# Weight transfers beside attention: issued by GpSimd's queue instead of SyncE's, with more lead counted for them

## The chip, the cores and the metric

The kernel runs on one core of a Trainium2 chip. Its engines are TensorE (PE, matrix products), VectorE (DVE), ScalarE (ACT), GpSimd (POOL) and SyncE (SP), which only issues transfers. Each engine takes its instructions strictly in the order in which the program has them; engines wait for each other, and for DMAs, on semaphores. 16 DMA engines move the data that any queue issues. The metric is the device time of one execution in microseconds; the median of the runs counts.

## The reference

```
attn = sigmoid(q @ k.T / sqrt(64) - log(448)) @ v         # 4 batches, 12 heads, 448 tokens, head size 64
x    = attn as (1792 tokens, 768)
h    = x @ moe_w_in;   x = elu(h) @ moe_w_out             # 768 -> 2048 -> 768
h    = x @ moe2_w_in;  out = (h - tanh(h)) @ moe2_w_out   # 768 -> 2048 -> 768
```

q, k and v come as float32, the four weights as float64, so a block of 128 x 768 weights is 768 KB.

## The kernel before

**Work.** Attention goes pair by pair of heads, 24 pairs, two of them per load. For a pair PE transposes q and k (`sps`, L309), splits of which ACT (L315) and DVE (L317, L322) write; it computes the scores (`sps`, `spq`, L344), ACT takes the sigmoids (`an`, `a`, L358), PE multiplies with v (`pvps`, L369) and DVE copies the result out (L381). After attention come the two layers. Every product there is made by a scheme with seven products in place of eight, from operands split into a high and a low part: `x_sum` (L702), `x_head` (L712) and `x_rest` (L718) make the operands of x, for tokens s = 0 and s = 1, and `m_p` (L746) runs the products of the first layer.

**Weights beside attention.** A float64 weight is made into float32 in three steps, `narrow_to`: ACT (L541), DVE (L544), DVE (L548). Beside attention this is done for the first four blocks of the first weight (`job(...)` with place 4, n = 0 to 3: `load` into the buffer `R1a`, `narrow`, and for n = 2 and 3 `keep` of the result in DRAM) and for all 16 blocks of the second weight: `p_load` (L592, into `XB` for even j and `XA` for odd j by the trace's names; j = 0 to 7, c = 0 and 1), `p_narrow`, four sums `p_sum` (L601), and two stores `p_store` (L606: 192 KB for c = 0 and 1152 KB for c = 1) into `p_forms` in DRAM. The buffers of j are used again by j + 2: `p_load` of j + 2 waits for the narrowing of j, and its narrowing waits for the stores and sums of j. When the last of this is done, the same space takes the operands of x for s = 0 (`x_head` and `x_rest` into `XB`).

**The order.** The class `Sched` writes the order out ahead of time. Each operation has a queue, a counted cost and a counted latency (`raw_op(key, queue, cost, fn, after, latency)`); operations go by earliest start, then by rank, and those of attention keep their own planned order. On ACT and DVE another operation is put into a gap only if it ends before the next planned one of attention, plus 100 ns. The counts only set the order; on the chip an instruction waits for its data alone. An entry in the list `after` that has no shared data, such as `("s", 1, 0)` for `p_load`, orders only the count.

GpSimd's work in this stretch is eight memsets and the mask `ident` at the start, ended at 3.4 us; its sums of weights (`w_sum`, L661) begin after attention.

Of the kernel before, what the change touches and what calls it, by code (L numbers as in the profile page):

```python
# [11 lines left out]
I32 = mybir.dt.int32  # L12
# [87 lines left out]
def kernel(  # L100
# [20 lines left out]
    nc = tc.nc  # L121
# [5 lines left out]
    SP = S // R  # L127
    NAN, NAF, NVL, NL = 3, 1, 2, 2
    KD = DM // 128
# [6 lines left out]
    DH = DM // 2  # L136
# [31 lines left out]
    with tc.manual_schedule():  # L168
# [246 lines left out]
        def mlp():  # L415
# [42 lines left out]
            def raw_tile(tag, epoch):  # L458

                if (tag, epoch) not in raws:  # L460
                    n = RAW[tag]
                    split = epoch % 2 == 1 and tag != "R1b"
                    raws[tag, epoch] = raw_p.tile([128, n], F32R if split else F32, tag=tag, name=tag)
                return raws[tag, epoch]
# [23 lines left out]
            CW = KD * 128  # L488
# [3 lines left out]
            wide = moe_w_in.dtype != F32  # L492
# [5 lines left out]
            kept, stage_of, in_scratch = {}, {}, set()  # L498
            OPENING = {0: 0, 1: 1} if wide else {}

            def stage(job):
                p, epoch = stage_of[job]
                if p >= 2:
                    return raw_tile(*{2: ("R1b", epoch), 4: ("R1a", 0), 5: ("R1a", 1.5)}[p])[:, :2 * CW]
                return (first[:, :2 * CW], second)[p]
# [7 lines left out]
            def result(job):  # L513
                if job in OPENING:
                    return spare[:, OPENING[job] * CW:(OPENING[job] + 1) * CW]
                return scratch(job) if job in in_scratch else stage(job)[:, :CW]

            def source(key):
                w, i, n = key
                f0 = n * 128  # L520
                if w == "wi":
                    return w_ins[i][:, f0:f0 + 128].bitcast(dt).rearrange("(k p) f -> p k f", p=128)
                return w_outs[i][f0:f0 + 128, :].bitcast(dt).rearrange("p (k f) -> p k f", k=KD)

            def load(job, key, narrowed):
                t = stage(job)
                if narrowed:
                    nc.sync.dma_start(out=t[:, :CW], in_=kept[key])
                elif wide:
                    nc.sync.dma_start(out=t.bitcast(I32).rearrange("p (k f) -> p k f", k=KD), in_=source(key))  # L530
                else:
                    nc.sync.dma_start(out=t[:, :CW].rearrange("p (k f) -> p k f", k=KD), in_=source(key))

# [19 lines left out]
            def keep(job, key):  # L553
                if key[:2] == ("wo", 1):
                    j, c = divmod(key[2], 2)
                    nc.sync.dma_start(out=w_forms()[:, 2 * c:2 * c + 2, j], in_=result(job).rearrange("p (r e) -> p r e", r=2))
                    return
                name = "kept_" + "_".join(map(str, key))
                kept[key] = store_p.tile([128, CW], F32, name=name, tag=name)
                nc.sync.dma_start(out=kept[key], in_=result(job))  # L560

            def w_forms():
                if "wf" not in hidden:
# [13 lines left out]
            def p_part(j, what):  # L577
                lo, hi = ((0, 2 * CW), (2 * CW, 4 * CW), (4 * CW, 5 * CW), (5 * CW, 8 * CW))[what]
                if j % 2 and what < 2:
                    return rooms["XA2"][:, lo:hi]  # L580
                return rooms["XB0"][:, lo + j % 2 * 4 * CW:hi + j % 2 * 4 * CW]
# [7 lines left out]

            def p_load(j, c):  # L590
                if wide:
                    nc.sync.dma_start(out=p_part(j, c).bitcast(I32).rearrange("p (k f) -> p k f", k=KD), in_=source(("wo", 0, 2 * j + c)))  # L592
                else:
                    nc.sync.dma_start(out=p_part(j, 2 + c)[:, :CW].rearrange("p (k f) -> p k f", k=KD), in_=source(("wo", 0, 2 * j + c)))

            def p_narrow(j, c, step):
                narrow_to(step, p_part(j, c), p_part(j, 2 + c)[:, :CW], p_part(j, 2 + c)[:, :CW])
# [5 lines left out]
            def p_store(j, c):  # L603
                t = p_part(j, 2 + c)
                a0, a1 = ((0, 1), (1, 7))[c]
                nc.sync.dma_start(out=p_forms()[:, a0:a1, j], in_=t[:, :(a1 - a0) * DH].rearrange("p (a e) -> p a e", a=a1 - a0))  # L606

            def p_forms():
                if "pf" not in hidden:
                    hidden["pf"] = store_p.tile([128, 7 * NG * DH], F32, name="p_forms", tag="p_forms")  # L610
                return hidden["pf"].rearrange("p (a j e) -> p a j e", a=7, j=NG)
# [205 lines left out]
            def o_order(i, s):  # L817
# [5 lines left out]
            W_SUMS = {"S1": ("A21", "A22", ALU.add), "S2": ("S1", "A11", ALU.subtract),  # L823
                      "S4": ("A12", "S2", ALU.subtract), "S3": ("A11", "A21", ALU.subtract)}
# [127 lines left out]
            def dve(n):  # L952
                return int(1.047 * n) + 150

            def raw_op(key, queue, cost, fn, after, latency=100):
                assert key not in mine, key
                mine[key] = (queue, cost, fn, list(after), latency)

            def op(kind, key, queue, cost, fn, after, latency=100):
                raw_op((kind,) + key, queue, cost, lambda: fn(*key), after, latency)  # L960
# [61 lines left out]
            t = 0  # L1022
# [10 lines left out]
            def job(key, keeps, place, after=(), only=False, i=0):  # L1033

                n = count[0]
                count[0] += 1
                stage_of[n] = (place, 2 * i + 1)
                if only and wide:
                    in_scratch.add(n)
                live = key not in kept_by  # L1040
                after = list(after) + list(stage_frees[place])
                if not live:
                    after.append(("keep", kept_by[key], key))
                raw_op(("load", n), "SP", 600, lambda: load(n, key, not live), after, 8500 if live else 6000)
                done = ("load", n)
                if place == 4:
                    fixed[done] = 3 * CYCLE + n
                free = scratch_free[(0, 0, 1, 2, 2, 3)[place]]
                if live and wide:
                    for step, (queue, cost) in enumerate((("ACT", 910), ("DVE", 560), ("DVE", 970))):  # L1050
                        raw_op(("narrow", n, step), queue, cost, lambda step=step: narrow(n, step),
                               [done] + (free if step == 0 else []), 100)
                        done = ("narrow", n, step)
                        if place == 4:
                            fixed[done] = n * CYCLE
                    free[:] = [done]
                stage_frees[place] = [done]
                if keeps:
                    kept_by[key] = n
                    raw_op(("keep", n, key), "SP", 600, lambda: keep(n, key), [done], 12000 if place == 4 else 5600)  # L1060
                    if n in in_scratch:
                        free[:] = [("keep", n, key)]
                    else:
                        stage_frees[place].append(("keep", n, key))
                return n, done
# [314 lines left out]
            for j in range(NG):  # L1380
                was = [] if j < 2 else [("p_narrow", j - 2, c, 2) for c in range(2)]
                held = [] if j < 2 else [("p_sum", j - 2, x) for x in W_SUMS] + [("p_store", j - 2, c) for c in range(2)]
                for c in range(2):
                    op("p_load", (j, c), "SP", 600, p_load, [("s", 1, 0)] + (was[c:c + 1] if wide else held), 11000)
                    done = ("p_load", j, c)
                    for step, (queue, cost) in enumerate((("ACT", 910), ("DVE", 560), ("DVE", 970)) if wide else ()):
                        op("p_narrow", (j, c, step), queue, cost, p_narrow,
                           [done] + (held if step == 0 else []), 100)
                        done = ("p_narrow", j, c, step)
                    ends_in[c] = done  # L1390
                both = [ends_in[c] for c in range(2)]
                for x in W_SUMS:
                    op("p_sum", (j, x), "DVE", dve(DH), p_sum, both + [("p_sum", j, y) for y in W_SUMS[x][:2] if y in W_SUMS])
                op("p_store", (j, 0), "SP", 600, p_store, both[:1], 8000)
                op("p_store", (j, 1), "SP", 600, p_store, both[1:] + [("p_sum", j, x) for x in W_SUMS], 8000)
            for k in mine:
                if k[0][:2] == "p_":
                    fixed[k] = (2 * k[1] + 2) * CYCLE
# [15 lines left out]
            for k, o in mine.items():  # L1414
                after = [x for a in o[3] for x in joint.get(a, [a])]
# [11 lines left out]
            while todo:  # L1427
                k = todo.pop()
# [47 lines left out]
```

## Time and profile before

| | us |
|---|---|
| median of 3 runs | 1025.57 (1024.84 to 1026.34) |
| the profiled execution | 1025.25 |
| its span, first to last instruction | 1023.5 |
| PE busy, of the span | 990.7 |
| DVE, ACT, POOL busy | 763.9, 600.8, 79.4 |
| mean granted TensorE clock | 0.992 of full speed |

Busy times are sums over the span, in which attention (to about 197 us) and the two layers have different limits; what a change in one stretch is worth is read in that stretch. Times in the rows are us from the start of the span, durations in us unless marked ns.

### The profile page before, as it was taken

The page shows a single profiled execution, that of the slowest core. Times are in us where ns is not written, and L with a number is a line of the kernel's source. Part 1 is how long each engine was busy: PE and PEld are TensorE (multiplying, and loading weights), DVE is VectorE, ACT ScalarE, POOL GpSimd, SP SyncE. Part 2 cuts the span into 40 slices and gives each one's busy share as a digit, 9 for nine tenths or more (in the row PEclk, how much of TensorE's full clock was granted, in tenths as well). Part 3 has the DMA queues.
Part 4 walks back from the last instruction along what each step waited for, and adds up shares of the span by engine and source line. Part 5 has one row for each costly group of instructions (what it writes and reads, how often), then busy time and mean ns, then how long its engine had stood idle before and what let it go on. Part 6 is the DMA issues. An engine that isn't in the chain of part 4 may idle for free.

```text
span 1023.5 us, 15546 instructions
## 1 busy us (share of the span) xinstructions
PE 990.7 (97%) x5300; PEld 855.4 (84%) x5300; DVE 763.9 (75%) x1155; ACT 600.8 (59%) x966; POOL 79.4 (8%) x74
## 2 busy tenths in 40 slices
PE   8969899989999999999999999999999999999998
PEld 6535455678888888888899998888888999999998
DVE  3657677898888888768878789777777779566673
ACT  4746567876666667666667565444444546445652
POOL 0000000012222220000000021111111000000000
PEclk9989899999999999999999999999999999999999
DMA  7889897025555569999994733555555894455442
GB/s 196 240 253 302 250 285 219 16 80 190 189 188 188 188 203 316 380 412 411 345 328 125 247 109 111 191 190 191 187 194 184 304 335 160 136 174 170 125 143 89
DMA packets 171263, 218.61 MB, mean 214 GB/s; under 512 B 58672, under 2 KB 129584, under 8 KB 170928
## 3 DMA queue, kind: packets, MB, share of 16 engines
q1 hardware_dynamic: 169616, 217.04, 63.8%
q8 instruction: 41, 0.67, 0.3%
q10 hardware_dynamic: 1568, 0.59, 0.2%
q14 instruction: 38, 0.31, 0.1%
HBM read 142.61 MB, written 74.97 MB: 213 GB/s over the span
## 4 chain that ended last, share of the span: by engine, by line
PE 89%; DMA 5%; DVE 3%; ACT 1%; issue 1%; SPq 1%; ACTq 0%; DVEq 0%
PE psa L746 12%; PE psd L746 11%; PE psx L746 9%; PE psu L901 7%; PE psv L901 7%; PE psw L901 7%; PE pvps L369 6%; PE psa L901 6%; PE psb L901 6%; PE psb L746 5%; PE psy L901 4%; PE sps L344 3%; PE psx L901 3%; DMA p_forms<-XB 2%; PE sps L309 2%; DMA R1a<-in_moe_w_in_dram 1%
## 5 line engine op out<-in xcount | busy, mean ns | idle before, releaser
L358 ACT ACTIVATE an<-sps,bias 128x896 f32<-128x896 f32 x72 | 67.3, 1005 | 34.1 <-PE sps L344 33.9
L873 ACT ACTIVATE XB<-t 128x384 fp32r<-128x384 f32 (+1 forms) x111 | 62.0, 563 | 40.8 <-PE psw L901 11.7
L877 DVE TENSOR_TENSOR XB<-t,XB 128x384 fp32r<-128x384 f32 (+1 forms) x111 | 68.3, 625 | 13.2 <-ACT XB L873 13.0
L661 POOL TENSOR_TENSOR second<-second 128x384 f32<-128x384 f32 x15 | 19.0, 1269 | 709.1 <-DVE second L548 213.6
L369 PE MATMUL pvps<-an,vl 128*64 128x448 f32 x288 | 62.7, 573 | 0.0
L873 ACT ACTIVATE XB<-spare 128x512 fp32r<-128x512 f32 (+1 forms) x72 | 41.1, 572 | 26.9 <-PE psw L901 6.6
L344 PEld LDWEIGHTS sps<-e 64*128 64x128 f32 x432 | 39.9, 189 | 18.9 <-PE pvps L369 15.5
L746 PE MATMUL psa<-XB,W 128*128 128x512 f32 x192 | 54.2, 391 | 0.0
L344 PE MATMUL sps<-e 64*128 64x448 f32 x432 | 51.3, 380 | 0.0
L877 DVE TENSOR_TENSOR XB<-spare,XB 128x512 fp32r<-128x512 f32 (+1 forms) x72 | 44.2, 621 | 9.2 <-ACT XB L873 8.8
L901 PE MATMUL psu<-XB,XB 128*128 128x384 f32 (+1 forms) x192 | 46.3, 348 | 0.0
L901 PE MATMUL psv<-XB,XB 128*128 128x384 f32 (+1 forms) x192 | 46.2, 348 | 0.0
L901 PE MATMUL psw<-XB,XB 128*128 128x384 f32 (+1 forms) x192 | 46.2, 348 | 0.0
L369 PEld LDWEIGHTS pvps<-an,vl 128*64 128x64 f32 x288 | 19.5, 144 | 28.5 <-issue 21.1
L746 PEld LDWEIGHTS psa<-XB,W 128*128 128x128 f32 x192 | 36.0, 188 | 7.5
L775 ACT ACTIVATE spare<-t 128x512 f32<-128x512 f32 (+1 forms) x33 | 19.0, 579 | 37.2 <-DVE t L763 36.1
L661 POOL TENSOR_TENSOR first<-first,second 128x384 f32<-128x384 f32 x30 | 40.1, 1335 | 1.2
L317 DVE CAST e<-sps 128x448 fp32r<-128x448 f32 x24 | 15.0, 624 | 30.4 <-PE sps L309 19.3
L746 PE MATMUL psd<-XB,W 128*128 128x512 f32 x144 | 35.7, 391 | 1.5 <-DVE W L678 1.3
L779 ACT ACTIVATE spare<-spare 128x512 f32<-128x512 f32 (+1 forms) x64 | 36.6, 572 | 0.7
L901 PE MATMUL psa<-XB,XB 128*128 128x384 f32 (+1 forms) x156 | 36.9, 347 | 0.0
L901 PE MATMUL psb<-XB,XB 128*128 128x384 f32 (+1 forms) x156 | 36.9, 347 | 0.0
(362 smaller groups left out, 2717.7 us busy)
## 6 DMA issues: line engine op xcount, KB each, us to landing
x_forms<-R1b SPq DMA_DIRECT2D x58, 256.0 KB, 2.0
first<-p_forms SPq DMA_DIRECT2D x36, 384.0 KB, 6.1
t<-x_forms SPq DMA_DIRECT2D x64, 192.0 KB, 2.9
t<-x_forms SPq DMA_DIRECT2D x47, 256.0 KB, 5.0
x_forms<-t SPq DMA_DIRECT2D x44, 256.0 KB, 2.0
x_forms<-R1b SPq DMA_DIRECT2D x58, 192.0 KB, 4.8
first<-in_moe_w_in_dram SPq DMA_DIRECT2D x14, 768.0 KB, 5.3
second<-in_moe_w_in_dram SPq DMA_DIRECT2D x14, 768.0 KB, 6.2
```

The source lines that it names most:

```text
L309: nc.tensor.transpose(ps[:, c * P:(c + 1) * P], t[:, c, h:h + 2, :], ident[:P, :P])
L317: nc.vector.tensor_copy(out=to, in_=x)
L344: nc.tensor.matmul(out=ps[:, j, :S], lhsT=e[lanes, ks, cols], rhs=e[lanes, qs, :S], start=(x == 0), stop=(x == 2),)
L358: nc.scalar.activation(out=a[:, :m], in_=T.pop(("s", n, u))[:, :m, :S], func=ACTF.Sigmoid, bias=bias, scale=scale)
L369: nc.tensor.matmul(out=ps[D * j:D * j + D], lhsT=vl[n // NL % NVL][:, n % NL, 5 * j + u if u < 3 else 3 + j], rhs=a[:, j if u < 3 else 0], ...
L661: by.tensor_tensor(out=out, in0=x, in1=y, op=op)
L746: nc.tensor.matmul(out=ps, lhsT=w[wz][:, k0:k0 + 128], rhs=xs[xz][:, kk], start=(opens and n == 0), stop=(n == 3 * KH - 1), skip_group_che ...
L775: nc.scalar.activation(out=r, in_=h, func=ACTF.Tanh)
L779: nc.scalar.activation(out=r, in_=r, func=ACTF.Exp, scale=-1.0)
L873: nc.scalar.activation(out=at_place(og_place[i, s, p, j], 0, i)[:, :HW[s]], in_=T["graw", i, s, p, j], func=ACTF.Copy)
L877: nc.vector.tensor_tensor(out=lo, in0=T.pop(("graw", i, s, p, j)), in1=f(hi), op=ALU.subtract)
L901: nc.tensor.matmul(out=T["o2", tag], lhsT=lhsT, rhs=rhs, start=(p in OPENS and j == 0 and x == 0), stop=(j == NG - 1 and x == 2), skip_gro ...
```

## The change

The 4 loads and 2 keeps with place 4 and all `p_load` and `p_store` are issued by `nc.gpsimd` instead of `nc.sync`. In the order they stand on the queue POOL with a cost of 1500 instead of 600, and with longer latencies: 14000 instead of 8500 for the loads with place 4, 12000 instead of 11000 for `p_load`, 9000 instead of 8000 for `p_store`. The loads and stores of q, k, v, of everything after attention, and the two loads that bring the kept blocks back stay on SyncE.

```
             def load(job, key, narrowed):
                 t = stage(job)
+                by = nc.gpsimd if stage_of[job][0] == 4 else nc.sync
...
-                    nc.sync.dma_start(out=t.bitcast(I32).rearrange("p (k f) -> p k f", k=KD), in_=source(key))
+                    by.dma_start(out=t.bitcast(I32).rearrange("p (k f) -> p k f", k=KD), in_=source(key))
...
             def keep(job, key):
...
-                nc.sync.dma_start(out=kept[key], in_=result(job))
+                (nc.gpsimd if stage_of[job][0] == 4 else nc.sync).dma_start(out=kept[key], in_=result(job))
...
             def p_load(j, c):
-                    nc.sync.dma_start(out=p_part(j, c).bitcast(I32)..., in_=source(("wo", 0, 2 * j + c)))
+                    nc.gpsimd.dma_start(out=p_part(j, c).bitcast(I32)..., in_=source(("wo", 0, 2 * j + c)))
...
             def p_store(j, c):
-                nc.sync.dma_start(out=p_forms()[:, a0:a1, j], in_=...)
+                nc.gpsimd.dma_start(out=p_forms()[:, a0:a1, j], in_=...)
...
-                raw_op(("load", n), "SP", 600, lambda: load(n, key, not live), after, 8500 if live else 6000)
+                raw_op(("load", n), *(("POOL", 1500) if place == 4 else ("SP", 600)), lambda: load(n, key, not live), after, 14000 if place == 4 else 8500 if live else 6000)
...
-                    raw_op(("keep", n, key), "SP", 600, lambda: keep(n, key), [done], 12000 if place == 4 else 5600)
+                    raw_op(("keep", n, key), *(("POOL", 1500) if place == 4 else ("SP", 600)), lambda: keep(n, key), [done], 12000 if place == 4 else 5600)
...
-                    op("p_load", (j, c), "SP", 600, p_load, [("s", 1, 0)] + (was[c:c + 1] if wide else held), 11000)
+                    op("p_load", (j, c), "POOL", 1500, p_load, [("s", 1, 0)] + (was[c:c + 1] if wide else held), 12000)
...
-                op("p_store", (j, 0), "SP", 600, p_store, both[:1], 8000)
-                op("p_store", (j, 1), "SP", 600, p_store, both[1:] + [("p_sum", j, x) for x in W_SUMS], 8000)
+                op("p_store", (j, 0), "POOL", 1500, p_store, both[:1], 9000)
+                op("p_store", (j, 1), "POOL", 1500, p_store, both[1:] + [("p_sum", j, x) for x in W_SUMS], 9000)
```

## Rows read from the trace of the kernel before

**Rows 1.** Page, part 1: busy time, share of the span, instructions of each engine.
```profile
PE 990.7 (97%) x5300; PEld 855.4 (84%) x5300; DVE 763.9 (75%) x1155; ACT 600.8 (59%) x966; POOL 79.4 (8%) x74
```

**Rows 2.** Chain of waits, 0 to 240 us: start, duration, what.
```profile
5.57 3.71 DMA first<-in_q_dram
...
15.18 3.16 PE pvps L369 x16
...
55.18 13.80 DMA R1a<-in_moe_w_in_dram
...
72.70 3.96 PE pvps L369 x16
...
91.83 9.74 DMA p_forms<-XB
...
108.27 11.31 DMA p_forms<-XB
...
168.58 3.16 PE pvps L369 x16
...
175.41 3.16 PE pvps L369 x16
...
194.21 3.18 PE pvps L369 x16
```

**Rows 3.** Windows: stretch, its length, busy time per engine, granted clock, DMA share, GB/s.
```profile
6.00:9.00 3.00, 1.67 (x12) 1.25 (x12) 1.27 (x3) 1.06 (x2) 0.00 (x0) 1.00 0.92 213
...
56.00:60.00 4.00, 4.00 (x26) 1.83 (x23) 3.23 (x6) 3.14 (x5) 0.00 (x0) 1.00 1.04 399
...
68.00:72.00 4.00, 1.16 (x6) 1.16 (x7) 2.08 (x4) 3.00 (x4) 0.00 (x0) 0.50 0.56 126
...
80.00:100.00 20.00, 19.96 (x131) 11.45 (x129) 15.91 (x28) 13.81 (x19) 0.00 (x0) 1.00 0.95 292
...
200.00:222.60 22.60, 18.49 (x90) 15.80 (x88) 22.46 (x39) 17.89 (x35) 5.12 (x4) 1.00 0.15 53
```

**Rows 4.** Waits, 0 to 245 us: total us, times, longest us.
```profile
POOL second L661 <- DVE XB L718: 199.6, 1, 199.6
...
ACT R1b L541 <- DMA R1a<-in_moe_w_in_dram: 12.0, 2, 9.2
ACT XB L541 <- DMA p_forms<-XB: 11.8, 4, 5.3
...
ACT XB L541 <- DMA XA<-in_moe_w_out_dram: 4.2, 2, 2.8
```

**Rows 5.** Timeline of SyncE's queue: start, duration, what, count.
```profile
19.95 1.45 SPq L592 DMA_DIRECT2D XB<-in_moe_w_out_dram  x2
...
56.31 9.98 SPq L234 DMA_DIRECT2D kq<-in_q_dram  x4
```

**Rows 6.** Timeline of PE, 190 to 245 us; in brackets the idle time before.
```profile
222.59 0.62 PE L746 MATMUL psd<-XB,R0a 128*128 128x384 f32 x2 [3.25 <-ACT R1b L758]
```

**Rows 7.** Timeline of DVE, 155 to 245 us.
```profile
161.81 0.62 DVE L317 CAST e<-sps 128x448 fp32r<-128x448 f32 x1 [0.69 <-PE sps L309]
163.10 1.22 DVE L322 TENSOR_TENSOR e<-sps,e 128x512 fp32r<-128x512 f32 x2 [0.66 <-ACT e L315]
165.01 0.63 DVE L381 COPY R1a<-pvps 128x448 f32<-128x448 f32 x1 [0.68 <-PE pvps L369]
...
172.36 1.88 DVE L718 TENSOR_TENSOR XB<-R0a,XB 128x512 fp32r<-128x512 f32 x3
```

**Rows 8.** Lines L606 and L234: durations of an issue in ns, min/median/max.
```profile
L606 SPq DMA_DIRECT2D p_forms<-XB x16: 378/539/1522, 38.9 to 166.1; - x16
...
L234 SPq DMA_DIRECT2D first<-in_q_dram x20: 435/816/3688, 12.3 to 147.2; - x20
```

**Rows 9.** DMA issues: count, KB each, median us from issue to landing.
```profile
p_forms<-XB SPq DMA_DIRECT2D x8, 1152.0 KB, 8.9
...
R1a<-in_moe_w_in_dram SPq DMA_DIRECT2D x4, 768.0 KB, 9.0
```

More of the change, by code (lines that the diff above doesn't have):

```diff
@@ L591, in p_load @@
                 if wide:
-                    nc.sync.dma_start(out=p_part(j, c).bitcast(I32).rearrange("p (k f) -> p k f", k=KD), in_=source(("wo", 0, 2 * j + c)))
+                    nc.gpsimd.dma_start(out=p_part(j, c).bitcast(I32).rearrange("p (k f) -> p k f", k=KD), in_=source(("wo", 0, 2 * j + c)))
                 else:
-                    nc.sync.dma_start(out=p_part(j, 2 + c)[:, :CW].rearrange("p (k f) -> p k f", k=KD), in_=source(("wo", 0, 2 * j + c)))
+                    nc.gpsimd.dma_start(out=p_part(j, 2 + c)[:, :CW].rearrange("p (k f) -> p k f", k=KD), in_=source(("wo", 0, 2 * j + c)))
             def p_narrow(j, c, step):
@@ L605, in p_store @@
                 a0, a1 = ((0, 1), (1, 7))[c]
-                nc.sync.dma_start(out=p_forms()[:, a0:a1, j], in_=t[:, :(a1 - a0) * DH].rearrange("p (a e) -> p a e", a=a1 - a0))
+                nc.gpsimd.dma_start(out=p_forms()[:, a0:a1, j], in_=t[:, :(a1 - a0) * DH].rearrange("p (a e) -> p a e", a=a1 - a0))
             def p_forms():
```

## The prediction, made before the result was known

> **What bounds the kernel now.** I read the page's busy table first: TensorE (PE) is busy 97% of the span, so only a stretch where it stands idle can give time back [rows 1]. The chain of waits shows where that is. Attention has a fixed beat: the `pvps` group of one pair of heads starts 6.83 us after that of the pair before (168.58 to 175.41); the last three beats take 18.80 together, since the last two pairs have no transposes beside them. The first group starts at 15.18, the last at 194.21. Undisturbed this takes 20 x 6.83 + 18.8 = 155.4 us; it took 179.0, so 23.6 us are lost. The same view names what stands there: DMAs of 13.80, 9.74 and 11.31 us, all of them weight transfers [rows 2]. A deep loss is followed by a slow group: with a granted clock of 0.50 in 68 to 72 us (1.2 instead of 2.4 GHz, after PE had stood still) the group at 72.70 took 3.96 instead of 3.16 [rows 2, 3]. That is inside the 23.6.
>
> The table of waits says how a late weight stops attention. ACT takes its work in the written order; it waits 12.0 us for `R1a` (loads of the first layer's weight), 11.8 for `p_forms` (stores of the second weight's parts, whose buffer the next narrowing writes) and 4.2 for `XA` (loads of the second weight), 28.0 in all [rows 4]. The sigmoids behind these narrowings come late, and so does PE.
>
> Why are they late? SyncE's own timeline shows one line for everything. The load into `R1a` issued at 55.18 lands 13.80 us later; the four q loads behind it hold SyncE for 9.98 us, where one takes 0.82 in the median [rows 2, 5, 8]. The DMA engines are full while weights flow (share 1.04 in 56 to 60 us) and half empty just after (0.56 in 68 to 72) [rows 3].
>
> After attention DVE is the bound: it is busy 22.46 of the 22.6 us ahead of 222.6 [rows 3], making operands for the first products. PE's last long stand (3.25 us) ends at 222.59 [rows 6]. This DVE work can begin only when the second weight has left the buffer `XB`; its first instruction `XB<-R0a` stands at 172.36 [rows 7]. So the end of the passage hangs on two things: when attention ends, and when the weights have left `XB`.
>
> **The change, part by part.**
>
> *Moved issues.* 4 loads and 2 keeps of the first weight, 16 loads and 16 stores of the second leave SyncE's queue for GpSimd's: 38 instructions. A store costs SyncE 0.54 us in the median [rows 8], so at most some 20 us of its time in all; SyncE bounds nothing, so this alone is worth nothing. What it buys is that q, k and v no longer queue behind weights, nor weights behind q, k and v.
>
> *GpSimd's cost of an issue.* No row shows GpSimd issuing a transfer. The nearest from below is a store's shortest issue on SyncE, 0.38 us; from above, the longest of all there, 3.69 us, a q load held up by a full queue [rows 8]. I take 0.54, that of the same store. Up to 3.69 it costs nothing: from the last memset (3.4 us) 38 issues behind each other and 8.9 us of landing [rows 9] end at 3.4 + 38 x 3.69 + 8.9 = 152.5 us, before the 167.6 that I come to below. What hides it is that GpSimd has nothing else to do: it sits idle for 199.6 us there [rows 4]. Above that the cover is gone, and GpSimd's pace sets the end (last rival).
>
> *Early issues.* The order holds the first loads of the second weight back until the scores of pair 1, but only on paper: their buffers are fresh, so no data makes them wait. On SyncE they stood behind all the first q, k and v loads and left at 19.95 [rows 5]. GpSimd has nothing in front of them, so load 0 of the first weight and then both halves of `p_load` 0 leave from 3.4 us on; load 1 stands behind narrowing 0 and holds back the rest. That is 3 x 768 KB = 2.36 MB into a stretch where the DMA engines have a share of 0.92 at 213 GB/s [rows 3], while PE waits for its first q load (5.57 to 9.28) [rows 2]. If that load keeps its time the cost is 0; if all 2.36 MB pass first, it is 8.1 us at the 292 GB/s of the slice 80 to 100 us [rows 3]. With equal shares, and weights flowing from 4.9 us, the 0.93 MB that passed until 9.28 would take as much of the weights along: 4 us, which I take.
>
> *More lead.* In the order a narrowing now stands 1500 + 12000 instead of 600 + 11000 ns behind its load, 1500 + 9000 instead of 600 + 8000 behind the store that frees its buffer (1.9 us more each), and 15.5 instead of 9.1 us behind a load of the first weight. The measured landings are 9.0 us for that load and 8.9 for the large store in the median [rows 9], so the new counts cover the usual case, though not all of a pile-up like 13.80 [rows 2]. ACT has one gap per beat for these, so a narrowing moves by no gap or by one. Two chains of three store-to-narrowing steps run interleaved (j = 0, 2, 4, 6 and 1, 3, 5, 7), so the weights leave `XB` 0 to 3 beats (0 to 20.5 us) later in the order. I take one beat, 6.8 us.
>
> *Stalls that remain.* The bytes are the same, so the engines stay near full; of 23.6 us I keep 8 (bounds 2, one short hold-up, and 23.6). Late next are the q and k loads: after 9.98 us of waiting for issue they would have been late too.
>
> *Sum.* Attention's last group lasts 3.1 us [rows 2], so attention ends at 15.2 + 155.4 + 4 + 8 + 3.1 = 185.7. The weights leave `XB`: all 23.6 us were lost ahead of 172.36, so undisturbed at 148.8; plus 6.8 + 4 + 8 = 167.6. From there DVE needed 50.2 us to the end of PE's stand (172.4 to 222.6). Attention's own share of DVE is 0.62 + 1.22 + 0.63 = 2.47 us per beat, 36% [rows 7]; it ran beside for 24.9 us before and 18.1 now, which saves 6.8 x 0.36 = 2.5. So PE goes on at 167.6 + 50.2 - 2.5 = 215.3 instead of 222.6: 7.3 us less. The profiled execution took 1025.25 us, its span of 1023.5 and 1.75 around it, 0.3 below the median of the runs (1025.57); 1025.3 - 7.3 = 1018.0.
>
> **Rivals.** *Better: the lead costs nothing.* If every narrowing finds its old gap and only 3 us of stalls remain, `XB` is free at 148.8 + 7 = 155.8 and attention ends at 180.7, both 16.6 us earlier: 1008.7. For it: the waits it must hide sum to 28 us, but few are long [rows 2, 4]. Against it: it needs the same bytes through in less time.
>
> *No change: the DMA engines were the bound.* In the slice from 80 to 100 us the share is 0.95 [rows 3]. If that is the limit, two queues move the bytes no faster, the same waits return in other places, and the early burst takes what little is won: 1024 to 1027. Against it: a share of 0.56 right after a pile-up, while other transfers still wait for issue. The Trainium skill's page "DMA: Bandwidth & Descriptors", section "Issuing engines are not separate DMA queues", says just this: all issuers end on the same 16 engines, and a second one saves only issue time. By that rule the time would stay as it is; the 9.98 us for four q issues speak against it here, the share of 0.95 for it.
>
> *Slower: attention's loads starve.* SyncE's single line also rationed the weights. With a queue of their own, their long rows can crowd out the 256-byte rows of q and k, first between 3.4 and 13 us, then behind each set of 2 x 768 + 192 + 1152 KB. PE then waits for transposes (L309) instead of for sigmoids. At 8.1 us for the start and 20 for the rest, attention ends at 173.7 + 28.1 = 201.8, `XB` is free at 155.6 + 28.1 = 183.7, and PE goes on at 183.7 + 50.2 - 2.5 = 231.4: 8.8 us more, 1034. It decides from 19.3 us of start and stalls together (the 12 taken and the 7.3 gained).
>
> *Slower: GpSimd sets the pace.* At 4.1 us per issue the end of 38 issues reaches 167.6; from 4.4 us (`XB` free at 179) the gain is gone; at 4.7 `XB` is free at 190.9, with no attention left beside DVE's work (24.9 x 0.36 = 9.0 us less), and PE goes on at 190.9 + 50.2 - 9.0 = 232.1: 1035. For it: it is the one unknown without a row of its own; against it: the nearest rows reach only to 3.69.
>
> **How the numbers follow.** Forecast 0.43, better 0.16, no change 0.14, starved loads 0.15, GpSimd's pace 0.12. A measurement of this kernel can tell about 0.2%, 2 us, from no change: faster 0.59, same 0.14, slower 0.27. The forecast's own range is 1013 to 1022 (no beat to two beats of lead, 6.8 x 0.64 = 4.4 us each). Eight times in ten: 1006, a little below the better case, to 1036, a little above the slower ones; I leave out 0.08 below and 0.11 above.
>
> **What would show it.** Right: one load into `R1a` and two into `XB` issued by GpSimd before 10 us; the first transposes at about 13 us instead of 9.4; SyncE's four q loads back at 2 to 4 us; ACT's waits for DMA under 10 us in sum; DVE's first `XB<-R0a` at 160 to 172; PE's last long stand ending near 215. Wrong: ACT still waiting over 20 us for DMA (no change); PE waiting for q or k at L309 in mid-attention (starved); a GpSimd issue over 4 us; or the first `XB<-R0a` after 175 us with attention long done, so that the lead costs more than the stalls did.

## The result and the profile after

The changed kernel took 1016.57 us in the median of 4 runs (1014.18 to 1017.18), the kernel before 1025.95 beside it (4 runs): a ratio of 0.9902, 95% interval 0.9878 to 0.9925. That is faster by 1.0%, and 1.4 us below the 1018.0 forecast. The profiled execution took 1016.46 us, its span 1013.8, 9.7 less than before. Lines from L525 on are numbered one higher here.

The page of the changed kernel, parts 1 and 3 (queue: packets, MB, share of 16 engines' span):

```profile
PE 988.3 (97%) x5300; PEld 856.7 (85%) x5300; DVE 763.6 (75%) x1155; ACT 602.0 (59%) x966; POOL 104.0 (10%) x112
...
q1 hardware_dynamic: 156464, 189.51, 56.4%
q0 software_dynamic: 5984, 27.53, 7.2%
```

PE's busy time fell by 2.4 us against [rows 1]: the span's 9.7 us are mostly idle time gone. POOL has 38 instructions more, the issues, and a queue of its own (q0).

GpSimd's timeline in the changed kernel (in brackets the idle time before, and what ended it):

```profile
3.33 1.00 POOL L531 DMA_DIRECT2D R1a<-in_moe_w_in_dram  x1
4.33 1.11 POOL L593 DMA_DIRECT2D XB<-in_moe_w_out_dram  x2
29.15 0.84 POOL L531 DMA_DIRECT2D R1a<-in_moe_w_in_dram  x1 [23.70 <-ACT an L358]
29.98 1.06 POOL L593 DMA_DIRECT2D XA<-in_moe_w_out_dram  x2
49.80 0.55 POOL L607 DMA_DIRECT2D p_forms<-XB  x1 [18.75 <-DVE XB L549]
```

The early issues came as forecast: one load into `R1a` and two into `XB` by 5.4 us, against 19.95 in [rows 5]. An issue costs GpSimd 0.54 to 1.05 us, not far from the 0.54 taken and well under the 4.1 from which GpSimd would have set the pace.

The chain of waits of the changed kernel, to be held against [rows 2]:

```profile
7.48 8.02 DMA kq<-in_q_dram
...
23.86 3.16 PE pvps L369 x16
...
80.18 4.55 SPq L217
...
87.81 5.08 DMA first<-in_k_dram
...
180.69 3.16 PE pvps L369 x16
```

Two things stand there. The first group begins at 23.86 instead of 15.18: 8.7 us are lost at the start, behind loads of q and k. The chain names a q load into `kq`, but the transposes that go on at 15.51 read `first`, and the k load into `first` issued at 4.2 us is the one that lands just ahead of them. From the first group to the last it took 156.83 us, where 155.4 is undisturbed: 1.4 us lost in the middle, where [rows 2] lost 23.6. What is left there is the late k loads of 80 to 93 us. The three weight transfers of 13.80, 9.74 and 11.31 us are gone from the chain.

What the weights did to that load stands in the DMA view of 4.3 to 4.5 us in the changed kernel (count, KB each, us from issue to landing):

```profile
XB<-in_moe_w_out_dram POOLq DMA_DIRECT2D x1, 768.0 KB, 8.1
first<-in_k_dram SPq DMA_DIRECT2D x1, 96.0 KB, 11.2
```

The k load of 96 KB took longer than the weight block of 768 KB issued 0.1 us after it; in the kernel before the same load, issued at the same time, landed after 3.5 us.

The waits of the changed kernel (total us, times, longest us), against [rows 4]; ACT has no row for a weight before 200 us any more:

```profile
POOL p_forms L607 <- DVE XB L549: 41.7, 8, 18.8
...
POOL R1a L531 <- ACT an L358: 24.3, 2, 23.7
...
PE sps L309 <- DMA kq<-in_q_dram: 8.6, 1, 8.6
```

GpSimd now waits for the narrowings that SyncE's issues waited for before, and nothing of attention's stands behind it in its line.

Windows (stretch, its length, busy time per engine PE, PEld, DVE, ACT, POOL, granted clock, DMA share, GB/s), against [rows 3]. First the changed kernel, then two stretches of the kernel before:

```profile
9.00:12.00 3.00, 0.00 (x0) 0.00 (x0) 0.30 (x1) 0.00 (x0) 0.00 (x0) 0.50 1.04 405
60.00:80.00 20.00, 20.00 (x135) 12.02 (x133) 16.94 (x29) 15.16 (x21) 5.82 (x9) 1.00 1.05 349
80.00:100.00 20.00, 18.51 (x126) 11.10 (x123) 15.14 (x26) 13.79 (x19) 3.02 (x5) 1.00 0.99 316
100.00:120.00 20.00, 20.00 (x133) 11.82 (x132) 17.05 (x32) 15.65 (x21) 4.82 (x8) 1.00 1.04 357
```
```profile
60.00:80.00 20.00, 12.19 (x75) 7.79 (x74) 8.87 (x15) 8.47 (x11) 0.00 (x0) 0.83 0.85 253
...
100.00:120.00 20.00, 15.55 (x90) 8.58 (x90) 11.35 (x20) 10.71 (x15) 0.00 (x0) 0.91 0.95 276
```

From 60 to 120 us the DMA engines moved 349, 316 and 357 GB/s. In the kernel before the same three windows read 253, 292 and 276. So they had not been at their limit before. The share alone does not tell this, since it read 0.85 to 0.95 before and reads 0.99 to 1.05 now: per busy time the engines also moved about a tenth more (an estimate, GB/s over share), and the packets changed with the issuer (last section). e9 below shows that this is not what freed attention. From 9 to 12 us they are full (405 GB/s) and PE does nothing, its granted clock at 0.50.

The end of the passage in the changed kernel, on the timelines of DVE and PE, answering [rows 7] and [rows 6]:

```profile
165.67 1.89 DVE L719 TENSOR_TENSOR XB<-R0a,XB 128x512 fp32r<-128x512 f32 x3
...
211.07 1.01 PE L747 MATMUL psd<-XB,R0a 128*128 128x384 f32 x2 [5.61 <-ACT R1b L759]
```

`XB` is free at 165.67 instead of 172.36, and PE goes on at 211.07 instead of 222.59: 11.5 us earlier, of which the span keeps 9.7. PE stood 5.61 us ahead of that instead of 3.25, and the first pair of matmuls after it took 1.01 us instead of 0.62. The windows of the 6 us that follow, of the changed kernel and of the kernel before, show why:

```profile
211.10:217.10 6.00, 6.00 (x19) 6.00 (x20) 4.34 (x8) 2.12 (x5) 0.00 (x0) 0.50 0.43 164
```
```profile
222.60:228.60 6.00, 5.13 (x26) 4.50 (x27) 5.78 (x11) 3.54 (x7) 0.00 (x0) 1.00 0.43 164
```

The granted clock was 0.50 (1.2 GHz) and not 1.00, and 19 matmuls were recorded instead of 26. That is the likely place of the 1.8 us that the span does not keep. The length of the stand does not settle it alone: PE stood 3.25 us in e8, e2 and e9 below, as in the kernel before, and the 6 us that followed had a granted clock of 0.75 in e8 and 1.00 in the other two.

### The profile page after: what moved, and what is told of

Same layout as the page of the kernel before. It is cut to its first block, busy times and chain, and to the rows that moved or that the text cites. A ratio compares the mean times of both kernels' runs of the same rounds, so it can differ in the third digit from the quotient of the medians.

```text
span 1013.8 us, 15564 instructions
## 1 busy us (share of the span) xinstructions
PE 988.3 (97%) x5300; PEld 856.7 (85%) x5300; DVE 763.6 (75%) x1155; ACT 602.0 (59%) x966; POOL 104.0 (10%) x112
## 3 DMA queue, kind: packets, MB, share of 16 engines
q1 hardware_dynamic: 156464, 189.51, 56.4%
q0 software_dynamic: 5984, 27.53, 7.2%
## 4 chain that ended last, share of the span: by engine, by line
PE 94%; DVE 2%; SPq 2%; DMA 1%; ACT 0%; issue 0%; DVEq 0%
PE psa L747 12%; PE psd L747 11%; PE psx L747 10%; PE pvps L369 7%; PE psu L902 7%; PE psv L902 7%; PE psw L902 7%; PE psa L902 6%; PE psb L902 6%; PE psb L747 5%; PE sps L344 5%; PE psy L902 4%; PE psx L902 3%; PE sps L309 2%; PE spq L344 2%; PE psd L902 1%
## 5 line engine op out<-in xcount | busy, mean ns | idle before, releaser
L369 PE MATMUL pvps<-an,vl 128*64 128x448 f32 x288 | 59.4, 548 | 0.0
L878 DVE TENSOR_TENSOR XB<-spare,XB 128x512 fp32r<-128x512 f32 (+1 forms) x72 | 44.2, 622 | 10.5 <-ACT XB L874 10.1
```

What stands on the lines that cost most here:

```text
L369: nc.tensor.matmul(out=ps[D * j:D * j + D], lhsT=vl[n // NL % NVL][:, n % NL, 5 * j + u if u < 3 else 3 + j], rhs=a[:, j if u < 3 else 0], ...
L878: nc.vector.tensor_tensor(out=lo, in0=T.pop(("graw", i, s, p, j)), in1=f(hi), op=ALU.subtract)
```

## The experiments

Eleven kernels, in three groups. Each ratio is to runs of the kernel before on the same chip (medians 1026.91, 1026.07 and 1028.32). For every trace I read the start of the first and last `pvps` group, DVE's first `XB<-R0a` and the moment PE goes on after its last long stand. One sum explains when `XB` comes free in all thirteen: 148.8 (undisturbed), plus the shift of the first group against 15.18, plus what attention lost (last minus first minus 155.4), plus 6.8 for each beat of lead.

| kernel | first, last group | lost | beats | `XB` by the sum | `XB` measured | PE goes on | us, ratio [95%] |
|---|---|---|---|---|---|---|---|
| before | 15.18, 194.21 | 23.6 | 0 | 172.4 | 172.36 | 222.59 | 1025.95 |
| after | 23.86, 180.69 | 1.4 | 1 | 165.7 | 165.67 | 211.07 | 1016.57, 0.9902 [0.9878, 0.9925] |
| e1 | 14.60, 175.57 | 5.6 | 2 | 167.4 | 167.33 | 207.88 | 1013.77, 0.9857 [0.9829, 0.9885] |
| e2 | 15.15, 180.26 | 9.7 | 0 | 158.5 | 158.42 | 208.64 | 1011.26, 0.9833 [0.9806, 0.9861] |
| e3 | 15.00, 191.57 | 21.2 | 1 | 176.6 | 176.55 | 222.58 | 1025.49, 0.9978 [0.9959, 0.9998] |
| e4 | 14.70, 175.35 | 5.3 | 2 | 167.2 | 167.11 | 207.67 | 1009.42, 0.9828 [0.9791, 0.9864] |
| e5 | 24.30, 182.71 | 3.0 | 1 | 167.7 | 167.68 | 213.65 | 1017.79, 0.9926 [0.9899, 0.9953] |
| e6 | 19.09, 178.28 | 3.8 | 1 | 163.3 | 163.25 | 209.23 | 1012.49, 0.9868 [0.9844, 0.9891] |
| e7 | 14.79, 177.14 | 7.0 | 0 | 155.4 | 155.29 | 205.46 | 1009.61, 0.9853 [0.9822, 0.9883] |
| e8 | 17.35, 173.08 | 0.3 | 0 | 151.3 | 151.23 | 201.46 | 1007.41, 0.9820 [0.9793, 0.9846] |
| e9 | 16.57, 187.93 | 16.0 | 0 | 166.2 | 166.08 | 216.31 | 1021.42, 0.9931 [0.9909, 0.9954] |
| e10 | 17.16, 179.14 | 6.6 | 1 | 164.2 | 164.12 | 210.04 | 1013.48, 0.9850 [0.9825, 0.9875] |
| e11 | 15.88, 171.53 | 0.3 | 0 | 149.8 | 149.68 | 199.91 | 1004.83, 0.9771 [0.9749, 0.9792] |

The beats are whole numbers chosen to fit, so the sum is a way of accounting for one trace, not a forecast; that whole beats fit to 0.1 us is what it shows. Two kernels were profiled twice: after and e5 lost 1.4 and 3.0 us, e8 and e11 0.3 and 0.3. So a difference of 1.6 us in that column can come from one execution to the next. The times of e8 and e11, the same kernel in two groups of runs, differ by 0.5% in their ratios, so a difference of that size between groups says little.

In e8 to e11 the first group begins 0.7 to 2.2 us later than in the kernel before. In e8 GpSimd issues q loads of the third group of heads from 10.68 us on, where SyncE had issued them from 12.29, and SyncE comes to the first weight at 15.48 instead of 19.95; which of the two costs the start was not tested.

**e1_held.** Both parts of the change, but the loads that no data holds back (load 0, `p_load` 0 and 1) stay with SyncE in code and order.

```diff
-                by = nc.gpsimd if stage_of[job][0] == 4 else nc.sync
+                by = nc.gpsimd if stage_of[job][0] == 4 and job else nc.sync
...
-                    nc.gpsimd.dma_start(out=p_part(j, c)...
+                    (nc.gpsimd if j >= 2 else nc.sync).dma_start(out=p_part(j, c)...
```

> The changed kernel, but the loads that have no data to wait for (load 0 of the first weight, p_load of j = 0 and 1) are issued by SyncE again, behind the first q, k and v loads, in code and in the order; all else as changed. Theory 'the early burst costs the start': the first pvps group, at 23.86 us in the changed kernel and 15.18 before, is back at 15 to 16, attention's later loss stays near 1.4 us, and the time falls by 6 to 9 us, to 1008 to 1011. Rival 'the burst is repaid': the 2.36 MB sent early must be sent later instead, a pile-up returns around 60 to 100 us with 5 us or more of waits, and the time stays at 1014 to 1017.

The first group came back to 14.60, so the early burst is what cost the start: 9.3 us against the changed kernel. The expectation is half missed: only 2.8 us of that stayed in the median (1013.77 against 1016.57 in another group of runs), between the two forecasts, and the later loss of over 5 us that the rival named came. PE went on 3.2 us earlier. The rest is accounted for: attention lost 5.6 instead of 1.4 in the middle, and the order found one beat more of lead for `XB`.

**e2_queue_only.** The order of the kernel before, untouched; GpSimd issues everything except those same first loads.

```diff
-                    nc.sync.dma_start(out=p_part(j, c)...
+                    (nc.gpsimd if j >= 2 else nc.sync).dma_start(out=p_part(j, c)...
...
-                nc.sync.dma_start(out=p_forms()[:, a0:a1, j], in_=t...
+                nc.gpsimd.dma_start(out=p_forms()[:, a0:a1, j], in_=t...
```

> The order of the kernel before, unchanged; GpSimd issues the weights beside attention (the first ones, as in e1_held, by SyncE). Theory 'the queue is the cause': ACT's waits for DMA fall from 28 us to under 10, attention's loss to under 10, time 1010 to 1017. Rival 'the counted lead is the cause': ACT still waits 20 us or more for weights, since the narrowings stand where they stood and the same bytes are in the way, time 1020 to 1026. Mixed: 10 to 20 us of waits, 1015 to 1021.

The queue alone gives 1.7%, more than the whole change. ACT's waits for weights are down to 2.6 us in one row (`XA`). What attention still loses, 9.7 us, now has another name in the chain of waits of e2:

```profile
47.09 11.92 DMA first<-in_k_dram
...
82.71 8.47 DMA vl<-in_v_dram
...
104.58 14.82 DMA first<-in_k_dram
```

The starved loads of the rival on record are there, in a mild form: they cost less than the stalls that went.

**e3_lead_only.** SyncE issues everything as before; only the counted times are those of the change.

```diff
-                    op("p_load", (j, c), "SP", 600, p_load, ..., 11000)
+                    op("p_load", (j, c), "SP", 600, p_load, ..., 12900)
...
-                op("p_store", (j, 0), "SP", 600, p_store, both[:1], 8000)
+                op("p_store", (j, 0), "SP", 600, p_store, both[:1], 9900)
```

> SyncE issues everything; only the order counts more lead (cost 600 plus 14900, 12900, 9900 and 12900, so that the sums are those of the changed kernel). Theory 'the queue is the cause': q, k and v still stand behind weights and weights behind them, attention loses 15 us or more, and the lead costs a beat (6.8 us) before XB is free: 1021 to 1028. Rival 'the counted lead is the cause': ACT's waits for DMA fall under 8 us, the start is as before, time 1009 to 1016.

The lead alone gives 0.2% (1025.49). It removes 2.4 of the 23.6 us lost and puts `XB` back by one beat. ACT's waits for weights fall from 28.0 to 15.3 us, the 12.0 here and 3.3 for `XA`; the row for `R1a` is gone. But DVE stands once for 14.4 us at a narrowing whose step ACT has yet to do, a kind of wait that e10 comes back to. The waits of e3:

```profile
DVE R1b L544 <- ACT R1b L541: 14.4, 1, 14.4
...
ACT XB L541 <- DMA p_forms<-XB: 12.0, 3, 5.8
```

**e4_waited.** All on GpSimd with the lead, but the first loads held back by data: a one-element copy of `e0` on GpSimd stands ahead of `p_load` 0, and load 0 comes after the scores of pair 1.

```diff
                 if wide:
+                    if (j, c) == (0, 0):
+                        nc.gpsimd.tensor_copy(out=warm, in_=f(e0)[:, 0, :1])
...
+                if place == 4 and not n:
+                    after.append(("s", 1, 0))
```

> The changed kernel with everything on GpSimd, but GpSimd's first load stands behind a copy of one element that DVE writes for pair 2 (some 18 us), so that the wait on attention, which was only in the order, is real. Theory 'the early burst costs the start': as e1_held, first pvps at 15 to 16 us, time 1008 to 1012. Rival 'the burst is repaid': 1014 to 1017.

Like e1, but with every issue on GpSimd: start at 14.70, 5.3 us lost, two beats, 1009.42. PE goes on within 0.2 us of e1. The medians differ by 4.4 us and the intervals overlap; I don't read a difference into them.

**e5_after_again and e6_wait_p.** The changed kernel again, and the changed kernel with its order kept and the copy of e4 ahead of `p_load` 0 alone; load 0 still leaves at 3.3 us.

```diff
                 if wide:
+                    if (j, c) == (0, 0):
+                        nc.gpsimd.tensor_copy(out=warm, in_=f(e0)[:, 0, :1])
```

> The changed kernel once more, to stand beside the three that follow: 1014 to 1018 us, first probabilities-times-v group at about 23.9 us, XB ready at about 165.7.

> The changed kernel, order and all, except that the two first expert-output loads (p_load of j = 0, 1.5 MB) stand behind a one-element copy on GpSimd that reads e0, so that they leave at about 9 us instead of 4.3; load 0 (0.75 MB) still leaves at 3.3. Theory 'the early burst costs the start': first group at 17 to 19 us instead of 23.9, later stalls 2 to 5 us instead of 1.4, XB with one beat of lead, time 1010 to 1014, some 3 to 6 us under the changed kernel. Rival 'what the start saves is lost later, as the same bytes only move': time within 1.5 us of the changed kernel.

With two of the three early loads held back the first group moved from 24.30 to 19.09, a little later than expected, and the time from 1017.79 to 1012.49; the intervals (0.9899 to 0.9953 and 0.9844 to 0.9891) don't meet. So the early burst costs the changed kernel about 5 us of its time, and the rival "what the start saves is lost later" is wrong: only 0.8 us more were lost in the middle than in e5.

**e7_wait_nolead.** e6 without the lead: the order of the kernel before, all weights on GpSimd, the copy ahead of `p_load` 0. Its diff against the kernel before is that of e2, without its two exceptions, and with the copy.

> The order of the kernel before, with every weight transfer beside attention issued by GpSimd and the first ones behind the one-element copy: the separate queue alone. Theory 'the queue does it, the counted lead costs a beat and buys fewer late q/k/v': like e2 (which left the first loads with SyncE), 1008 to 1013 us, later stalls 8 to 11 us, XB at 157 to 160. Rival 'the counted lead is what frees attention': ACT's waits for weights come back (over 10 us) and the time is over 1020.

1009.61. Attention lost 7.0 us, a little less than expected, `XB` came free at 155.29, before the 157 to 160 expected, and ACT waited 0.8 us for a weight. The rival that the lead is what frees attention falls here for the second time. Against e6 the lead buys 3.2 us of attention's loss, twice what two profiles of one kernel differ by, and pays a beat of `XB` for it; the times, 2.9 us apart, overlap in their intervals. Yet SyncE's line, with no weight in it now, is still slow with four q loads, on its timeline in e7:

```profile
20.55 0.80 SPq L256 DMA_DIRECT2D vl<-in_v_dram  x1
21.45 7.94 SPq L234 DMA_DIRECT2D kq<-in_q_dram  x4
```

**e8_swap and e11_swap_again.** The other way round: the order of the kernel before, weights left with SyncE, and the q, k and v loads from the third group of heads on (the code's `m` of 2 and more) issued by GpSimd.

```diff
-                    nc.sync.dma_start(
-                        out=ql[m % 2]...
+                    (nc.gpsimd if m > 1 else nc.sync).dma_start(
+                        out=ql[m % 2]...
```

> The order of the kernel before, weights left with SyncE, q, k and v loads from the third head on issued by GpSimd instead. Theory 'two lines instead of one': the weights no longer wait behind q/k/v, so ACT's waits for weights fall from 28 to under 8 us and the time is 1008 to 1016. Rival 'GpSimd's line serves what stands in it more slowly, and only the weights had room for that': q/k/v land later than in the kernel before, PE's waits for them are over 15 us, and the time is at or above 1022.

> e8 once more beside the two: 1005 to 1010 us, PE without a wait for a load of over 2 us after 20 us, last probabilities-times-v group at about 175.7.

This is the best of all: 1007.41, and 1004.83 in the last group of runs, 2.3% under the kernel before (0.9749 to 0.9792), just below what I expected of it. The chain of waits of e8 shows attention undisturbed, 155.73 us from first group to last:

```profile
17.35 3.16 PE pvps L369 x16
...
173.08 1.39 PE pvps L369 x7
```

The estimate of 148.8 for an undisturbed `XB` in the prediction is met too: 149.68 in e11, whose first group is 0.7 later. GpSimd's issues of q loads into `kq` (ns, min/median/max, in e8) are all alike, where SyncE's in e7 range from 330 to 3451:

```profile
L234 POOL DMA_DIRECT2D kq<-in_q_dram x20: 707/707/735, 24.2 to 136.1; - x20
```

**e9_both_pool.** Is it the separation, or is GpSimd simply the better issuer? Here weights (as in e2) and q, k, v (as in e8) stand in one line again, GpSimd's.

> The order of the kernel before, with the weights beside attention and the q, k and v loads from the third group of heads on all issued by GpSimd, so that they share one line again, GpSimd's instead of SyncE's. Theory 'two lines instead of one': the hold comes back, ACT waits over 10 us for weights or PE over 8 us for q/k/v, attention loses 12 us or more and the time is 1014 to 1026. Rival 'what was slow is SyncE's way of issuing small-row loads (53,680 packets for 17.1 MB where GpSimd's queue shows 5,920 for 13.8 MB), and any queue of GpSimd's is a cure': hardly any wait comes back, as in e8, and the time is 1004 to 1011.

1021.42: 16.6 us slower than e11 beside it, with 16.0 us lost in attention. The issuer alone is no cure; the separation is. The DMA engines were not the limit either: from 60 to 120 us, where the changed kernel had a share of 0.99 to 1.05, e9 has 0.85, 0.82 and 0.77. ACT waits for weights again, among others in this row of e9:

```profile
ACT XB L542 <- DMA p_forms<-XB: 7.3, 3, 5.6
```

The window of 100 to 120 us in e9:

```profile
100.00:120.00 20.00, 17.62 (x98) 9.82 (x98) 13.25 (x23) 11.95 (x17) 14.35 (x23) 0.84 0.77 252
```

GpSimd's timeline in e9 shows what holds its line, because there the hold is a wait with a name:

```profile
50.28 0.56 POOL L593 DMA_DIRECT2D XB<-in_moe_w_out_dram  x1
51.02 0.56 POOL L607 DMA_DIRECT2D p_forms<-XB  x1 [0.18 <-issue]
51.56 0.53 POOL L593 DMA_DIRECT2D XA<-in_moe_w_out_dram  x1
52.15 0.84 POOL L531 DMA_DIRECT2D R1a<-in_moe_w_in_dram  x1
53.66 2.14 POOL L234 DMA_DIRECT2D kq<-in_q_dram  x3 [0.67 <-issue]
57.88 0.71 POOL L234 DMA_DIRECT2D kq<-in_q_dram  x1 [2.08 <-PE sps L344]
59.67 1.50 POOL L217 DMA_DIRECT2D kq<-in_k_dram  x2 [1.09 <-DMA XB<-in_moe_w_out_dram]
62.08 0.75 POOL L217 DMA_DIRECT2D kq<-in_k_dram  x1 [0.91 <-DMA XA<-in_moe_w_out_dram]
64.77 1.34 POOL L225 DMA_DIRECT2D kq<-in_k_dram  x2 [1.94 <-DMA R1a<-in_moe_w_in_dram]
```

Count back from each k load that waits. The first (59.67) has four q loads, `R1a`, `XA` and `p_forms` ahead of it; the eighth back is `XB`, and `XB` is what it waits for. The third (62.08) waits for `XA`, again its eighth; the next (64.77) for `R1a`, its eighth. In e9 this holds for every wait of GpSimd's line for a landing, 17 of them between 30 and 160 us, 26.8 us in sum: its issues use eight landing semaphores in turn, and an issue stands until the transfer that used its semaphore last, eight places ahead in its own line, has landed. With weights and small loads mixed, k waits for weights that it does not use; and since the line is in order, the next weight waits behind k. In two lines a k load has only small loads eight places ahead of it.

SyncE's slow issues in the kernel before are another hold. A wait of SyncE for a landing would show in its own table of waits, as it does in e7:

```profile
SPq L217 <- DMA vl<-in_v_dram: 2.9, 5, 1.4
```

The same table of the kernel before, from 20 to 160 us, has no row with a DMA. The first q load at 56.31 [rows 5] has a v load eight places ahead of it that had landed at 52.44. For all 26 issues of SyncE over 1.5 us between 15 and 165 us the transfer eight ahead had landed, at least 1.79 us before the issue began. The time passes inside the issue. What ends it there stays open; e7 shows that it needs no weight in the same line.

**e10_swap_lead.** e8 with the lead of e3.

> e8 (q, k and v from the third group on issued by GpSimd, weights by SyncE) with the lead of e3 counted for the weights. Theory 'lead is paid by one beat of XB, of which the end follows 0.29': attention ends as in e8 at 174 to 177 us, XB comes at about 158 instead of 151.2, PE goes on 2 us later, 1.5 to 3 us more than e8. Rival 'the end follows XB in full': 6 to 8 us more than e8.

A miss: 1013.48 against 1004.83 of e11, 8.6 us more where I expected 1.5 to 3. The end does not follow `XB` in full either (14.4 us later, PE 10.1). My expectation took attention to end as in e8; it lost 6.6 us, 5.9 of them in one place (the two beats from 99.87 to 119.43 took 19.6 us instead of 13.7), which DVE's timeline and PE's wait in e10 explain:

```profile
108.56 0.65 DVE L544 TENSOR_SCALAR R1b<-R1b 128x768 int32<-128x768 int32 x1 [5.83 <-ACT R1b L541]
```
```profile
PE pvps L369 <- DVE R1a L381: 4.2, 1, 4.2
```

DVE stood 5.83 us at a narrowing whose first step ACT had behind the sigmoids of one pair of heads; DVE's copies out of PSUM (L381) stood behind it, and PE behind those. No DMA is in it: the lead moves narrowings into places where the written orders of ACT and DVE cross. With that loss in, one beat in `XB` and the 1.3 us later start, the sum of the table holds (164.2 against 164.12).

## Why the prediction was right, point by point

*What bounds the kernel*: right. The loss was attention's, caused by weights that came late because they shared SyncE's line with q, k and v. The half that is shown is weights behind q, k and v: SyncE's slow issues go on in e7 without weights in its line, so that q, k and v were held by weights ahead of them is not shown, nor is the prediction's "full queue". e2, e7 and e8 take the sharing away in three ways and gain 1.5 to 2.3%; e9 puts it back in another queue and loses most of that; e3 leaves it and gains 0.2%.

*GpSimd's cost of an issue*: 0.54 taken, 0.54 to 1.05 measured; GpSimd stood idle between its issues.

*Early issues*: the term was mis-sized. 4 us taken, 8.7 measured, above even the upper bound of 8.1. The weights did not share equally with the first small loads, they went ahead of them (11.2 us for 96 KB of k beside 8.1 for 768 KB of weights). PE's second set of transposes came 7.6 us late (15.51 instead of 7.87), and PE worked at a granted clock of 0.50 on top, until after 21 us, where the kernel before had 1.00 again by 13. e6 shows that about 5 us of the changed kernel's time hang on it.

*Stalls that remain*: mis-sized the other way, 8 taken and 1.4 measured, below the bound of 2. The reason I gave for keeping them, engines near full with the same bytes, failed: in the same windows they moved up to 357 GB/s instead of 292. But 1.4 belongs to the changed kernel as it starts; without the burst 3.8 to 5.6 are lost (e1, e4, e6). The two errors cancelled by luck: 12 taken, 10.1 measured.

*More lead*: one beat taken, one beat measured, to 0.1 us. So the last group began at 180.69, 1.9 us earlier than the 182.6 in the sum, and `XB` came free at 165.67 for 167.6.

*DVE's work after attention*: mis-sized. Each us less of overlap with attention was to save 0.36 us between `XB` and PE's going on; it saved about 0.7. From `XB` to PE it took 50.2 us before, with 24.9 of attention beside it (to the end of its last group), 45.4 in the changed kernel with 18.2, and 40.6 in e1 with 11.4: 4.8 us less per 6.8, twice. With that share, PE's going on is 0.71 times the shift of attention's end plus 0.29 times the shift of `XB`: 222.59 - 0.71 x 13.52 - 0.29 x 6.69 = 211.05 for 211.07; for e10, not used in the fit, 209.5 for 210.04. e3, e5, e6 and e10, with the overlap of the changed kernel, took 45.9 to 46.0 us, so the share is good to about a tenth. That DVE also has work after attention that does not need `XB` would explain it; I did not isolate it.

*The clock after the stand* was missing from the sum. PE worked 6 us at a granted clock of 0.50 after it, and 1.8 of the 11.5 us went back. Another 0.9 lies around the span (2.66 us instead of 1.75). So 211.07 instead of 215.3 became 1016.5 instead of 1018.0. That the forecast came within 1.4 us is again luck in part: PE went on 4.2 us earlier than in the sum, and 2.7 of that was lost behind it.

*The rivals.* "The DMA engines were the bound" is refuted by the 349 and 357 GB/s, and by e9, which loses 16.0 us with a lower share. The Trainium skill's "DMA: Bandwidth & Descriptors", section "Issuing engines are not separate DMA queues", says that a second issuer saves only issue time, usually a small one; by that rule the time would have stayed. The measurement goes against it: four q loads held SyncE for 9.98 us [rows 5], and all that stood behind them in its line came that much later. "Attention's loads starve" is seen in a mild form (e2): without the lead attention still loses 7 to 10 us, with the start as before, under the 19.3 from which it decides. "GpSimd's pace" did not come near.

## What to carry to other kernels

When big and small transfers share one issuing engine, look at how long the small ones hold that engine and what stands behind them in its line: if it is something that the kernel waits for, give the two kinds separate lines before touching the order. Look also at what each issue waits for: where a transfer a fixed number of places ahead has to land first, a mixed line is slow however cheap an issue is (e9). Try both ways round: here both gained, and though attention lost 7.0 us one way and 0.3 the other, the times side by side (1009.6 and 1007.4, 1004.8 again later) overlap in their intervals. A transfer moved to an idle queue leaves at once unless data holds it, so see what it meets at the start; and lead counted for transfers is paid in the steps of the schedule it is rounded to.

## What the runs showed of the hardware

The same bytes make other packets from another issuer, as the profile counts packets. The weights' 27.53 MB are 5,984 packets on GpSimd's queue, while SyncE's queue lost 13,152 in giving them up (169,616 to 156,464). For q, k and v the difference is larger, on the DMA view of the first 200 us of e7 (first fence: SyncE has q, k, v and almost nothing else) and of e8 (second: GpSimd has most of q, k, v, SyncE the weights and the rest):

```profile
q0 software_dynamic: 5984, 27.53, 37.2%
q1 hardware_dynamic: 53680, 17.08, 34.7%
```
```profile
q1 hardware_dynamic: 21520, 31.36, 45.4%
q0 software_dynamic: 5920, 13.77, 22.2%
```

So a packet holds 4.6 KB of weights beside 0.32 KB of q, k, v in e7, and 1.46 KB beside 2.33 KB in e8, where the 1.46 mixes weights with the first q, k and v loads; by the 13,152 packets above, weights alone make about 2.1 KB each from SyncE (an estimate). The Trainium skill's "DMA: Bandwidth & Descriptors", section "Queues, rings and completion order", says that a DMA engine takes turns between queues a packet at a time. If the packets of the profile are those of that section, which no run shows, q, k and v would by that get about a fourteenth of the weights' bytes per turn in e7 and more than theirs in e8, which fits k landings of up to 14.82 us in e2 and an attention without loss in e8. It fits, but no run here varies the packet alone, and SyncE's slow issues in e7 (7.94 us for four) would do for a cause as well. Which of the two lets attention lose 7.0 us in e7 and 0.3 in e8 stays open.
